# Grouped-query attention with a gated expert layer: the gate matrix in the start-up, earlier requests for the last weights, and the last output columns as separate products

## The chip, the cores and the metric

The kernel runs on one core of a Trainium2 chip. The core has five engines that each work through a queue of their own in order: TensorE (PE in the profile; its weight loads are PEld), VectorE (DVE), ScalarE (ACT), GpSimd (POOL) and SyncE (SP). Transfers run on sixteen DMA engines and are asked for by SyncE, ScalarE or GpSimd. The metric is the device time of one execution in microseconds (us). Before the change it is 369.04 us, the median of three runs (368.49 to 369.7).

## The reference

Attention over 8 batches of 384 positions, 16 query heads that share 4 key and value heads, 64 elements a head. Its output, regrouped to 3072 rows of 1024, goes into a two-stage gate: a row picks one of 4 groups and in it one of 4 experts, and is multiplied with that expert's two 1024 x 1024 matrices.

```python
scores = scale * np.matmul(q, k.transpose(0, 1, 3, 2))
attn = softmax(scores)                       # over the keys
x = np.matmul(attn, v)                       # then (batch, position) x 1024
g_idx = np.argmax(x @ w_group, axis=1)       # one of 4 groups
e_idx = np.argmax(xg @ w_expert[g], axis=1)  # one of 4 experts of the group
h = np.maximum(xg[mask_e] @ w1[g, e], 0.0)
out[tok_idx] = (g_w * e_w)[:, None] * (h @ w2[g, e])
```

## The kernel before

**Batches.** The eight batches run one after the other. For each batch `b` the kernel guesses one expert from the mean of v, loads that expert's two matrices `w1` and `w2` (4 MB each in float32, 2 MB each once they are cast to bf16 on the way), and computes the whole batch with it. Rows that chose another expert get weight zero and are left for a loop at the end, which runs once for each pair of a batch and an expert that is left over.

**Attention of a batch** (`Attn`) has 24 units: 4 key heads times 6 slices of the keys. In each unit TensorE computes scores of the unit after next (line 305), ScalarE takes the exp (line 311), TensorE multiplies with v (line 324), GpSimd adds pairs of exps (line 331) and VectorE reduces them to row sums (line 338). `run` takes a table of inserts: functions that are called after a given unit.

**The expert layer of a batch** has two halves. `moe_h(b, f0, ...)` computes two of the eight 128-column slices of the hidden layer (16 products, line 600) and ScalarE empties the tile (line 604). `ffn_y` and `y_out` compute the output (line 611), scale it with the rows' weights and store it. The layer of batch `b` runs after the attention of batch `b + 1`, in `block(b + 1)`; for batch 7 it stands alone at the end.

**Order of work.** The order is written out by hand: each engine does its work in the order in which the program names it. What matters here is the order in three queues.

- GpSimd: the adds of a batch's attention, then `prefetch(b)`: it reads the picked index (`pick`), makes a copy that waits until the q of batch `b + 1` has been transposed (`transposed`, line 667), and asks for `w1` (line 538) and `w2` (line 544) of batch `b`, then for k (line 92) and q (line 97) of batch `b + 2`.
- SyncE: the transposes by DMA of k and q of the next batch (lines 126, 128 and 120), loads of v (line 102), stores of results (lines 640 and 881).
- TensorE: its products in the order of the text.

There are two buffers each for `w1`, `w2` and v, and thirteen for the exps.

**Accumulator tiles.** `ps_tile` hands out four tiles of two banks: "s" and "o" each alternate between two, and "x" names the "o" tile that isn't the current one. A new product into a tile waits until the engine that reads the tile's old content is done.

**Start-up.** `first_scores` does warming products on a tile of ones (`fill`, line 268, 512 columns each), casts and transposes the first k and q on TensorE (lines 249 and 257), and copies them out. `gate_matrix_a` and `gate_matrix_b` bring the two gate matrices into the form that the gate needs: four transposes of float32 (line 221), two VectorE operations (lines 223 and 227), and later one product (line 232). Before the change part a stands after unit 3 of the attention of batch 0.

**The end.** The last loop over `c` computes three blocks of 128 rows, each as two halves of 512 columns. The very last half is emptied by ScalarE (256 columns, line 873) and VectorE (256 columns, line 874) and stored by SyncE and ScalarE (line 881).

Of the kernel before, what the change touches and what calls it, by code (L numbers as in the profile page):

```python
# [10 lines left out]
BF16 = mybir.dt.bfloat16  # L11
I32 = mybir.dt.int32
AX = mybir.AxisListType
ALU = mybir.AluOpType
# [4 lines left out]
def kernel(  # L19
# [11 lines left out]
    nc = tc.nc  # L31
# [39 lines left out]
    def ps_tile(which, shape=None, dtype=F32):  # L71
        if which == "x":
            which = f"o{1 - turn['o']}"
        else:
            turn[which] = 1 - turn[which]
            which += str(turn[which])
        return psum.tile(shape or [P, 2, 512], dtype, name="ps_" + which)
# [18 lines left out]
        qraw[b] = lpool.tile([P, KQ, NC * D], BF16, name="q_raw")  # L96
        nc.gpsimd.dma_start(out=qraw[b], in_=rows(q[b]))

    def load_v(b):
        vraw[b] = vpool.tile([P, Hkv, NC * D], F32, name="v_raw")  # L100
        for r in range(2):
            nc.sync.dma_start(out=vraw[b][r * H2:(r + 1) * H2],
                              in_=v[b].rearrange("h (p c) d -> p h (c d)", c=NC))

    def new_qT(b):
# [40 lines left out]
                              in_=v[0, g0:g1].rearrange("h (p c) d -> p h (c d)", c=NC))  # L146

    onesb = cpool.tile([P, 4 * P], BF16)
    nc.vector.memset(onesb, 1.0)
    nc.sync.dma_start(out=k0f[:, 0], in_=rows(k[0])[:, 0])  # L150
    for m in range(KG):
# [59 lines left out]
        nc.vector.tensor_scalar(eback, eidx, -1.0, float(NE - 1), op0=ALU.mult, op1=ALU.add)  # L211
        nc.vector.tensor_copy(out=pidx, in_=pback_i)

    gm = {}

    def gate_matrix_a(which):
        gm["pt"] = ps_tile(which, [P, 2, 512])
        pe = gm["pt"][:, 0, :Eg * 5 * KQ].rearrange("p (e n) -> p e n", e=Eg)
        wv = wraw.rearrange("a (p e) -> a e p", e=Eg)
        for e in range(Eg):  # L220
            nc.tensor.transpose(out=pe[:, e], in_=wv[:, e, :],
                                identity=id128f[:5 * KQ, :5 * KQ])
        nc.vector.tensor_copy(
            out=wg[:, :, :NW].rearrange("p k (a e) -> p e a k", e=Eg),
            in_=pe.rearrange("p e (a k) -> p e a k", k=KQ))
        pk = pe.rearrange("p e (a g t) -> p t g a e", a=5, t=KG)[:, 0]
        nc.vector.tensor_add(out=wgs.rearrange("p g (a e) -> p g a e", e=Eg), in0=pk,
                             in1=wg[:, 1::2, :NW].rearrange("p g (a e) -> p g a e", e=Eg))

    def gate_matrix_b():  # L230
        p2 = gm["pt"][:, 1, :Hkv * NW].rearrange("p (g n) -> p g n", n=NW)
        nc.tensor.matmul(out=p2, lhsT=mod64.rearrange("p a m -> p (a m)"), rhs=wgs,
                         start=True, stop=True)
        nc.vector.tensor_copy(out=wgd, in_=p2)
# [9 lines left out]
    def first_k(gp, which, eng):  # L244
        lo = gp * NC
        pt = ps_tile(which, [P, 16, P], BF16)
        for i in range(NC):
            for s in range(2):
                nc.tensor.transpose(out=pt[s * D:(s + 1) * D, i, :], in_=k16[0][:, lo + i],
                                    identity=id128b)  # L250
        evac(eng, kT[0][:, lo:lo + NC, :], pt[:, :NC, :])

    def first_q(i0, n, which, eng):
        pt = ps_tile(which, [P, 16, P], BF16)
        for i in range(n):
            a, c = (i0 + i) // SC, (i0 + i) % SC
            nc.tensor.transpose(out=pt[:, i, :], in_=qraw[0][:, a, c * P:(c + 1) * P],
                                identity=id128b)
        evac(eng, qT[0][:, i0:i0 + n, :], pt[:, :n, :])

    def first_scores():
        new_kT(0)
        new_qT(0)
        warm = ps_tile("o")

        def fill(n):
            for i in range(n):
                nc.tensor.matmul(out=warm[:, i % 2, :], lhsT=onesb[:, :P], rhs=onesb, start=True,  # L268
                                 stop=True)

        fill(8)
        nc.vector.tensor_copy(out=k16[0][:, :NC].rearrange("p c d -> p (c d)"), in_=k0f[:, 0])
        nc.scalar.copy(out=qraw[0][:, 0], in_=q0f[:, 0])
        nc.vector.tensor_copy(out=qraw[0][:, 1], in_=q0f[:, 1])
        first_k(0, "s", nc.vector)
        fill(2)
        first_q(0, SC, "s", nc.scalar)
        first_q(SC, SC, "o", nc.vector)
        fill(2)
        return fill  # L280

    def cast_k():
        nc.gpsimd.tensor_copy(out=k16[0][:, NC:NK].rearrange("p c d -> p (c d)"), in_=k0f[:, 1])
# [117 lines left out]
            out=rsum[b][:, g0:g1].rearrange("p g t j -> p g (t j)"),  # L401
            in_=reds[b][:, g0:g1].rearrange("p g n t j -> p g (t j) n"), axis=AX.X, op=ALU.add)

    def sums(b, g0, g1, which):
        sm = ps_tile(which, [P, Hkv, KG, NB])
        for r in range(2):
            for t in range(2):
                nc.tensor.matmul(out=sm[t * D:(t + 1) * D, g0:g1, r, :], lhsT=half32[:, r, :],  # L408
                                 rhs=rsum[b][:, g0:g1, t, :], start=True, stop=True)
        if b not in inv:  # L410
            inv[b] = gpool.tile([P, KQ, NB], F32, name="inv")
        nc.vector.reciprocal(out=inv[b][:, KG * g0:KG * g1],
                             in_=sm[:, g0:g1].rearrange("p g r j -> p (g r) j"))
# [213 lines left out]
    def moe_h(b, f0, which, mid=None):  # L627
        if f0 == 0:
            hTs[b] = xpool.tile([P, FQ, S], BF16, name="hT", bufs=1)
        ffn_h(xb[b], w1s[b], hTs[b], f0, which, mid)  # L630
# [14 lines left out]
    def do(f, *a):  # L645
        return lambda: f(*a)
# [1 line left out]


    gate_constants()  # L650
    fill = first_scores()
    index_constants()
    at = {0: Attn(0), 1: Attn(1)}
    at[0].start()
    fill(4)
    state, weights = {}, {}

    new_qT(1)
# [30 lines left out]
    def transposes(b):  # L689
        new_qT(b)  # L690
        trans_k(b)
        trans_q(b, 0, Hkv)
# [8 lines left out]
    def first_spread():  # L701
# [3 lines left out]
    a = at[0]  # L705
    a.run(0, NU, {
        1: [do(first_q, GB, GB, "x", nc.vector)],
        3: [cast_k, do(gate_matrix_a, "x")],
        4: [gate_matrix_b],
        6: [do(collect, 0, 0, 1)],  # L710
        7: [do(first_q, 2 * GB, 2 * GB, "x", nc.vector)],
# [22 lines left out]
        13: [do(cast, 0, 3)],  # L734
    })
    moe_h(0, 0, "s")
    load_v(2)
    transposes(2)
    pt = ps_tile("x")
    gate_logits(0, pt)  # L740
    guess_mean(1, pt)
    vm = mean_copy(pt, nc.scalar)
    moe_h(0, 2, "s", do(sums, 1, 0, 2, "s"))
    guess_logits(vm, pt)
    for m in range(2):
        normalise(1, m)
# [39 lines left out]
    def prefetch(b):  # L786
        if b != 2:
            pick(b)
        if b + 1 < B:
            transposed(b + 1)  # L790
        pick_w1(b)
        pick_w2(b)
        if b + 2 < B:
            loads(b + 2)

    def block(b):
        last = b == B - 1
        f = b - 1
        prefetch(b)
        moe_h(f, 0, "s")  # L800
        collect(b, 0, Hkv)
        weights[f]()
        out_weights(f)
        moe_h(f, 2, "s")
        sums(b, 0, Hkv, "o")
        for m in range(4):
            normalise(b, m)
        moe_h(f, 4, "s")
        moe_h(f, 6, "s")
# [12 lines left out]
        ffn_y(w2s[f], hTs[f], 1, "s", (1,), y)  # L822
        y_out(f, 1, y)
        if not last:
            guess_logits(vm, pt)
        weights[b] = gate_softmax(b, pt, not last)
        y = ffn_y(w2s[f], hTs[f], 2, "o", (0,))
        if not last:
            pick_index(b + 1)
            at[b + 1] = Attn(b + 1)  # L830
            y_scores(f, at[b + 1], y)
            return {}
        ffn_y(w2s[f], hTs[f], 2, "o", (1,), y)
        y_out(f, 2, y, nc.vector)
        weights[b]()
        out_weights(b)

    late = first_block()
    for b in range(2, B):
        if b + 1 < B:  # L840
            transposes(b + 1)
        at[b].run(0, NU, late)
        late = block(b)

# [17 lines left out]

    for c in range(SC):
        ot = opool.tile([P, DM], F32, name="ot")
        for nh in range(2):
            y = ps_tile("so"[nh])
            ffn_y(w2s[B - 1], hTs[B - 1], c, "", (nh,), y)
            sl = slice(nh * HALF, (nh + 1) * HALF)
            w = weff[B - 1][:, c:c + 1]
            if (c, nh) == (SC - 1, 1):  # L870
                q1 = slice(HALF, HALF + HALF // 2)
                q2 = slice(HALF + HALF // 2, DM)
                nc.scalar.mul(ot[:, q1], y[:, nh, :HALF // 2], w)
                nc.vector.tensor_scalar(ot[:, q2], y[:, nh, HALF // 2:], w, None, op0=ALU.mult)
            elif nh:
                nc.vector.tensor_scalar(ot[:, sl], y[:, nh, :], w, None, op0=ALU.mult)
            else:
                nc.scalar.mul(ot[:, sl], y[:, nh, :], w)
            for i, (ps, x) in enumerate(halves(c)):
                eng = nc.scalar if (c, nh, i) == (SC - 1, 1, 1) else nc.sync  # L880
                eng.dma_start(out=out_rows(out[(B - 1) * S:])[x][:, sl], in_=ot[ps, sl])
    region.close()

    n_left = nc.values_load(left_i[0:1, 0:1], min_val=0, max_val=B * NE)
# [72 lines left out]
```

The softmax here doesn't subtract the row's maximum and nothing guards it: scores larger than these inputs give would overflow.

## Time and profile before

| | value |
|---|---|
| time, median of three runs | 369.04 us |
| span of the profiled execution | 369.5 us |
| exp on ScalarE, 192 times | 814 ns each, 150.2 us |
| v products on TensorE (line 324), 1536 | 153.1 us busy |
| hidden-layer products (line 600), 480 on the "s" tiles | 81.1 us busy |
| weights asked for by GpSimd, 16 loads | 2048 KB each, median 22.6 us to landing |
| moved by DMA | 76.07 MB, mean 206 GB/s |

How to read it: busy time is summed over the span for each engine and says nothing of what waits for what. A line of the list of waits names the engine and the line that waited, after the arrow what ended the wait, then the total in microseconds, how often, and the longest. A line in order of time has start, duration, engine, source line, operation, tile written and tile read, and in brackets the idle time before it with what ended it. A row of a stretch of time gives each engine's busy time, then the granted TensorE clock, the busy share of the DMA engines (which can exceed 1, as transfers overlap) and what they moved in GB/s. In the chain that ended last each row is a start, a duration and the work that was followed back.

### The profile page before, as it was taken

Reading aid. Unit: us, or ns where it says so; the run is one execution under the profiler, and the core shown is the slowest. Engines: PE = TensorE matmul, PEld = TensorE weight load, DVE = VectorE, ACT = ScalarE, POOL = GpSimd, SP = SyncE. Lnnn points to the kernel's source line nnn. Section 1 sums busy time; section 2 is a strip of 40 time slices with the busy share of each in tenths; the row PEclk is TensorE's granted clock in tenths of the full one; section 3 lists DMA queues with packets and bytes.
Section 4 is the critical chain, followed back from the end, with each engine's and each line's share of the span. In section 5 each row is a group of like instructions: output and inputs, shape, how many; then the busy total and the mean of one; then the engine's idle time right before and its main releaser. Section 6 shows DMA issues by size and latency. Waiting matters only on the chain.

```text
span 369.5 us, 9587 instructions
## 1 busy us (share of the span) xinstructions
PE 357.0 (97%) x3984; PEld 185.7 (50%) x3999; DVE 259.2 (70%) x499; ACT 228.7 (62%) x300; POOL 150.0 (41%) x118
## 2 busy tenths in 40 slices
PE   8999999999999999999999999999999999999982
PEld 3545465455555455554555554554555545555530
DVE  4599799658976599747979379755997379793130
ACT  3889943749925596357944599355963589443221
POOL 6566960706803276034730377006750067500000
PEclk9999999999999999999999999999999999999997
DMA  8995999999999999999999999989999899999834
GB/s 195 247 105 88 241 213 159 248 235 287 219 155 201 256 263 211 131 201 285 234 208 154 259 261 213 193 134 243 281 212 186 157 227 240 212 212 266 230 76 98
DMA packets 71212, 76.07 MB, mean 206 GB/s; under 512 B 35928, under 2 KB 50264, under 8 KB 71168
## 3 DMA queue, kind: packets, MB, share of 16 engines
q0 software_dynamic: 26640, 41.03, 62.5%
q1 hardware_dynamic: 44096, 33.81, 37.6%
q8 instruction: 32, 0.52, 0.5%
q10 hardware_dynamic: 432, 0.61, 0.5%
q14 instruction: 12, 0.10, 0.1%
HBM read 89.21 MB, written 18.87 MB: 293 GB/s over the span
## 4 chain that ended last, share of the span: by engine, by line
PE 81%; DMA 9%; DVE 4%; ACT 2%; issue 1%; POOL 1%; POOLq 0%; ACTq 0%
PE ps_o L324 28%; PE ps_s L600 17%; PE ps_s L611 13%; DMA w<-in_moe_w_dram 9%; PE ps_s L305 8%; PE ps_o L611 7%; PE ps_o L444 3%; PE ps_o L268 2%; DVE red L338 1%; POOL e L331 1%; ACT e L311 1%; PE ps_o L408 1%; PE ps_o L454 1%; DVE ps_o L419 1%; DVE xT L428 1%
## 5 line engine op out<-in xcount | busy, mean ns | idle before, releaser
L311 ACT ACTIVATE e<-ps_s 128x768 f32<-128x768 f32 x192 | 150.2, 814 | 18.6 <-PE ps_s L305 15.6
L324 PE MATMUL ps_o<-e,v_raw 64*64 64x384 f32 x1536 | 153.1, 482 | 0.2 <-DVE xT L428 0.2
L331 POOL TENSOR_TENSOR e<-e 128x768 f32<-128x768 f32 x64 | 116.1, 1831 | 78.6 <-ACT e L311 54.4
L338 DVE TRANSPOSE_TENSOR_REDUCE red<-e 128x24 f32<-128x768 f32 x128 | 114.3, 947 | 18.3 <-POOL e L331 18.2
L600 PE MATMUL ps_s<-xb,w 128*128 128x384 bf16 x480 | 81.1, 326 | 1.0 <-ACT hT L604 0.8
L324 PEld LDWEIGHTS ps_o<-e,v_raw 64*64 64x64 f32 x1536 | 55.5, 133 | 37.4 <-issue 26.6
L600 PEld LDWEIGHTS <-w 128*128 128x128 bf16 x512 | 48.9, 98 | 36.7 <-issue 4.5
L305 PE MATMUL ps_s<-qT,kT 64*64 64x384 bf16 x768 | 63.7, 326 | 0.4 <-ACT e L311 0.2
L604 ACT ACTIVATE hT<-ps_s 128x768 bf16<-128x768 f32 x30 | 24.3, 810 | 62.0 <-PE ps_s L600 62.0
L611 PEld LDWEIGHTS <-hT 128*128 128x128 bf16 x384 | 36.0, 98 | 43.6 <-issue 3.6
L611 PE MATMUL ps_s<-w,hT 128*128 128x512 bf16 x234 | 54.6, 379 | 2.1 <-DMA w<-in_moe_w_dram 1.2
L305 PEld LDWEIGHTS <-kT 64*64 64x64 bf16 x768 | 24.4, 105 | 38.4 <-issue 36.7
L667 POOL COPY after<-qT 128x1 bf16<-128x1 bf16 x7 | 1.3, 192 | 86.4 <-DMA qT<-q_raw 83.5
L636 ACT ACTIVATE ot<-ps_s,we 128x1024 f32<-128x1024 f32 x14 | 15.6, 1114 | 27.3 <-PE ps_s L611 27.3
L611 PE MATMUL ps_o<-w,hT 128*128 128x512 bf16 x135 | 31.9, 379 | 0.1
L419 DVE STREAM_TRANSPOSE rb<-inv 128x384 f32<-128x384 f32 x60 | 31.0, 554 | 0.3
L428 DVE TENSOR_TENSOR xT<-xT,rb 128x768 f32<-128x768 f32 x25 | 24.0, 958 | 0.9
L240 ACT CAST xb<-xT 128x768 bf16<-128x768 f32 x27 | 21.1, 828 | 0.0
L374 DVE COPY xT<-ps_o 128x768 f32<-128x768 f32 x18 | 16.5, 919 | 0.0
L242 DVE CAST vm<-ps_o 128x4 bf16<-128x4 f32 x6 | 1.0, 161 | 21.0 <-PE ps_o L454 21.0
L638 DVE TENSOR_SCALAR ot<-ps_o,we 128x1024 f32<-128x1024 f32 x7 | 9.0, 1282 | 5.3 <-PE ps_o L611 5.1
L376 ACT COPY xT<-ps_o 128x768 f32<-128x768 f32 x10 | 8.0, 800 | 6.5 <-PE ps_o L324 6.5
(123 smaller groups left out, 181.3 us busy)
## 6 DMA issues: line engine op xcount, KB each, us to landing
w<-in_moe_w_dram POOLq DMA_DIRECT2D x16, 2048.0 KB, 22.6
out_dram<-ot SPq DMA_DIRECT2D x42, 256.0 KB, 7.8
xb_scratch<-xb SPq DMA_DIRECT2D x8, 768.0 KB, 10.2
q_raw<-in_q_dram POOLq DMA_DIRECT2D x7, 768.0 KB, 34.4
v_raw<-in_v_dram SPq DMA_DIRECT2D x14, 384.0 KB, 5.9
out_dram<-ot SPq DMA_DIRECT2D x11, 128.0 KB, 2.3
k<-in_k_dram POOLq DMA_DIRECT2D x7, 192.0 KB, 31.4
w<-in_q_dram POOLq DMA_DIRECT2D x3, 192.0 KB, 6.6
```

The lines of the kernel that those rows point to most:

```text
L240: eng.copy(out=out_, in_=in_)
L305: nc.tensor.matmul(out=sT[r * H2:(r + 1) * H2, s, :S], lhsT=kT[b][s * D:(s + 1) * D, slot, ks], rhs=qT[b][s * D:(s + 1) * D, kq * SC:(kq + ...
L311: nc.scalar.activation(e.rearrange("p t (s x) -> p s t x", s=2), sT[:, :, :S].rearrange("p s (t x) -> p s t x", t=2), ACT.Exp, scale=scale)
L324: nc.tensor.matmul(out=oT[t * D:(t + 1) * D, r, :S], lhsT=vraw[b][r * H2:(r + 1) * H2, g, c * D:(c + 1) * D], rhs=self.e[u][r * H2:(r + 1) ...
L331: eng.tensor_add(out=self.e[u], in0=self.e[u], in1=self.e[u + 1])
L338: nc.vector.tensor_reduce(out=reds[self.b][:, g, n].rearrange("p t j -> p (t j)"), in_=self.e[u].rearrange("p t (j x) -> p (t j) x", x=32) ...
L374: nc.vector.tensor_copy(out=dst, in_=src)
L419: nc.vector.transpose(out=rb[:, r].rearrange("p (j x) -> p j x", x=32), in_=inv[b][:, 2 * m + r].unsqueeze(2).to_broadcast([P, NB, 32]))
L428: eng.tensor_mul(out=x, in0=x, in1=rb)
L600: nc.tensor.matmul(out=h[:, jj, :S], lhsT=w1[:, kq, (f0 + jj) * P:(f0 + jj + 1) * P], rhs=x[:, kq, :], start=(kq == 0), stop=(kq == KQ - 1))
L604: nc.scalar.activation(hT[:, f0:f0 + 2, :], h[:, :, :S], ACT.Relu)
L611: nc.tensor.matmul(out=y[:, nh, :], lhsT=hT[:, f, c * P:(c + 1) * P], rhs=w2[:, f, nh * HALF:(nh + 1) * HALF], start=(f == 0), stop=(f == ...
```

## The change

It does five things.

1. **Start-up.** A second, smaller tile of ones (128 columns) is set first, and four products of 128 columns on it and six of 512 take the place of eight of 512. The fills between and after the transposes are three instead of four. ScalarE instead of VectorE copies out the first keys, VectorE instead of ScalarE the first queries. The idea is to have the first scores sooner.
2. **Gate matrix.** Part a moves from after unit 3 of batch 0 to directly after the first two scores, where four warming products stood, so that useful work keeps TensorE busy there.
3. **Row sums.** `sums` takes a piece of a tile that is handed in. For the first half of batch 1 that is the gate's tile, so no "s" tile is used up between two calls of `moe_h`.
4. **Requests.** v of batch 2 is asked for by GpSimd instead of SyncE, and the weights of batch 7 at the head of that batch's attention instead of after it.
5. **The end.** The last 512 columns become two groups of 256 with products of their own. VectorE empties the first, ScalarE the second, and SyncE stores both.

```diff
+    ones1 = cpool.tile([P, P], BF16)
+    nc.vector.memset(ones1, 1.0)
...
-        fill(8)
+        for i in range(4):
+            nc.tensor.matmul(out=warm[:, i % 2, :P], lhsT=ones1, rhs=ones1, start=True, stop=True)
+        fill(6)
...
-        first_k(0, "s", nc.vector)
-        fill(2)
-        first_q(0, SC, "s", nc.scalar)
+        first_k(0, "s", nc.scalar)
+        first_q(0, SC, "s", nc.vector)
+        fill(1)
         first_q(SC, SC, "o", nc.vector)
         fill(2)
...
     at[0].start()
-    fill(4)
+    gate_matrix_a()
...
-        3: [cast_k, do(gate_matrix_a, "x")],
+        3: [cast_k],
...
-    load_v(2)
+    load_v(2, nc.gpsimd)
...
-    moe_h(0, 2, "s", do(sums, 1, 0, 2, "s"))
+    moe_h(0, 2, "s", do(sums, 1, 0, 2, pt))
...
     def block(b):
...
-        prefetch(b)
+        if not last:
+            prefetch(b)
...
         if b + 1 < B:
             transposes(b + 1)
+        else:
+            prefetch(b)
         at[b].run(0, NU, late)
...
-        for nh in range(2):
-            y = ps_tile("so"[nh])
-            ffn_y(w2s[B - 1], hTs[B - 1], c, "", (nh,), y)
...
+        parts = [(0, HALF), (HALF, DM)]
+        if c == SC - 1:
+            parts = [(0, HALF), (HALF, 3 * HALF // 2), (3 * HALF // 2, DM)]
+        for i, (n0, n1) in enumerate(parts):
+            y = ps_tile("so"[i % 2])
+            for f in range(FQ):
+                nc.tensor.matmul(out=y[:, 0, :n1 - n0], lhsT=hTs[B - 1][:, f, c * P:(c + 1) * P],
+                                 rhs=w2s[B - 1][:, f, n0:n1], start=(f == 0), stop=(f == FQ - 1))
...
+            for ps, x in halves(c):
+                nc.sync.dma_start(out=out_rows(out[(B - 1) * S:])[x][:, n0:n1], in_=ot[ps, n0:n1])
```

More of the change, by code (lines that the diff above doesn't have):

```diff
@@ L97, in load_q, with load_v @@
         nc.gpsimd.dma_start(out=qraw[b], in_=rows(q[b]))
-    def load_v(b):
+    def load_v(b, eng=nc.sync):
         vraw[b] = vpool.tile([P, Hkv, NC * D], F32, name="v_raw")
         for r in range(2):
-            nc.sync.dma_start(out=vraw[b][r * H2:(r + 1) * H2],
+            eng.dma_start(out=vraw[b][r * H2:(r + 1) * H2],
                               in_=v[b].rearrange("h (p c) d -> p h (c d)", c=NC))
@@ L212, in index_constants, with gate_matrix_a @@
         nc.vector.tensor_copy(out=pidx, in_=pback_i)
[L214 to L218, printed above, removed]
+    def gate_matrix_a():
+        pe = ps_tile("o")[:, 0, :Eg * 5 * KQ].rearrange("p (e n) -> p e n", e=Eg)
         wv = wraw.rearrange("a (p e) -> a e p", e=Eg)
@@ L230, in gate_matrix_b @@
     def gate_matrix_b():
-        p2 = gm["pt"][:, 1, :Hkv * NW].rearrange("p (g n) -> p g n", n=NW)
+        p2 = ps_tile("x")[:, 1, :Hkv * NW].rearrange("p (g n) -> p g n", n=NW)
         nc.tensor.matmul(out=p2, lhsT=mod64.rearrange("p a m -> p (a m)"), rhs=wgs,
@@ L274, in first_scores @@
         nc.vector.tensor_copy(out=qraw[0][:, 1], in_=q0f[:, 1])
-        first_k(0, "s", nc.vector)
-        fill(2)
-        first_q(0, SC, "s", nc.scalar)
+        first_k(0, "s", nc.scalar)
+        first_q(0, SC, "s", nc.vector)
+        fill(1)
         first_q(SC, SC, "o", nc.vector)
         fill(2)
-        return fill
     def cast_k():
@@ L402, in collect, with sums @@
             in_=reds[b][:, g0:g1].rearrange("p g n t j -> p g (t j) n"), axis=AX.X, op=ALU.add)
-    def sums(b, g0, g1, which):
-        sm = ps_tile(which, [P, Hkv, KG, NB])
+    def sums(b, g0, g1, pt):
+        if isinstance(pt, str):
+            pt = ps_tile(pt)
+        sm = pt[:, 1, 128:128 + Hkv * KG * NB].rearrange("p (g r j) -> p g r j", r=KG, j=NB)
         for r in range(2):
@@ L650 @@
     gate_constants()
-    fill = first_scores()
+    first_scores()
     index_constants()
@@ L864 @@
         ot = opool.tile([P, DM], F32, name="ot")
-        for nh in range(2):
-            y = ps_tile("so"[nh])
-            ffn_y(w2s[B - 1], hTs[B - 1], c, "", (nh,), y)
[L868 to L876, printed above, removed]
-            else:
[L878 to L881, printed above, removed]
+        w = weff[B - 1][:, c:c + 1]
+        parts = [(0, HALF), (HALF, DM)]
[6 more added lines that the diff above has]
+                                 rhs=w2s[B - 1][:, f, n0:n1], start=(f == 0), stop=(f == FQ - 1))
+            if i % 2:
+                nc.vector.tensor_scalar(ot[:, n0:n1], y[:, 0, :n1 - n0], w, None, op0=ALU.mult)
+            else:
+                nc.scalar.mul(ot[:, n0:n1], y[:, 0, :n1 - n0], w)
+            for ps, x in halves(c):
+                nc.sync.dma_start(out=out_rows(out[(B - 1) * S:])[x][:, n0:n1], in_=ot[ps, n0:n1])
     region.close()
```

## The prediction

> **What bounds the kernel now.** I read the shares of the page first, then the waits, then GpSimd's order of time, then how long each load took to land, then the chain. The shares and the waits:
>
> ```profile
> PE 357.0 (97%) x3984; PEld 185.7 (50%) x3999; DVE 259.2 (70%) x499; ACT 228.7 (62%) x300; POOL 150.0 (41%) x118
> ...
> POOL after L667 <- DMA qT<-q_raw: 83.5, 6, 20.4
> ...
> PE ps_s L611 <- DMA w<-in_moe_w_dram: 1.2, 1, 1.2
> PE ps_s L600 <- ACT hT L604: 0.8, 1, 0.8
> ...
> SPq L102 <- PE ps_s L305: 6.2, 1, 6.2
> ```
>
> TensorE (PE) is at work 97% of the span and hardly waits: 1.6 us at the start, 0.8 us once at L600, 1.2 us once at L611. But GpSimd waits six times, 83.5 us in all, for the transposed q of the next batch (L667), and only after that copy does it ask for a batch's weights. In order of time:
>
> ```profile
> 70.25 0.19 POOL L667 COPY after<-qT 128x1 bf16<-128x1 bf16 x1 [0.69 <-DMA qT<-q_raw]
> 70.92 0.91 POOL L538 DMA_DIRECT2D w<-in_moe_w_dram  x1 [0.49 <-issue]
> ...
> 115.43 0.19 POOL L667 COPY after<-qT 128x1 bf16<-128x1 bf16 x1 [13.08 <-DMA qT<-q_raw]
> ...
> 294.91 0.22 POOL L667 COPY after<-qT 128x1 bf16<-128x1 bf16 x1 [20.39 <-DMA qT<-q_raw]
> 295.52 0.92 POOL L538 DMA_DIRECT2D w<-in_moe_w_dram  x1 [0.39 <-issue]
> ```
>
> From batch 1 to 6 the asks lie (295.52 - 70.92) / 5 = 44.9 us apart, while the chain has TensorE's batches 43.04 us apart (first L600 products at 102.27, 145.31, 188.35 us). The wait of the copy grows from 0.69 to 20.39. So there are two loops, and the transfers are the slower by 1.9 us a batch. The slack, from each load's time to landing against the first product that reads it (w1: L600, w2: L611):
>
> | batch | w1 lands, is read | w2 lands, is read |
> |---|---|---|
> | 1 | 93.6, 102.2 | 103.3, 112.9 |
> | 3 | 182.8, 188.3 | 192.8, 199.0 |
> | 5 | 271.9, 274.4 | 282.5, 285.1 |
> | 6 | 315.4, 317.4 | 326.4, 328.1 |
> | 7 | 336.3, 340.0 | 352.1, wanted at 350.7 |
>
> The slack shrinks from 9 us to nothing, and the last w2 comes 1.4 us late. Here the chain turns into a transfer:
>
> ```profile
> 318.41 33.72 DMA w<-in_moe_w_dram
> 352.13 0.04 issue
> 352.17 0.38 PE ps_s L611
> ```
>
> That row starts at the ask, but the ask didn't bound it. By stretch of time:
>
> ```profile
> 320.00:325.00 5.00, 5.00 (x38) 2.97 (x36) 3.11 (x10) 1.73 (x3) 0.00 (x0) 1.00 1.12 212
> ```
>
> The last two columns, DMA share 1.12 and 212 GB/s, stay near that from 305 to 345 us. Batch 6's w2 landed at 326.4, batch 7's w1 at 336.3, 9.9 us later for 2 MB: 212 GB/s, one after the other with no gap, though w1 was asked for at 317.5. **The end is bound by when the stream of weights began, not by the last ask.**
>
> **What the Trainium skill says.** "DMA: Bandwidth & Descriptors", Queues, rings and completion order: each DMA engine takes descriptors of a ring in order and goes round the rings that have work. The trace agrees: GpSimd's loads land in the order asked, and share only with SyncE's. The same page, SWDGE vs HWDGE vs iDMA: one queue is allocated for GpSimd's DMAs, so batch 7's weights asked for sooner stand behind batch 6's. "TensorE: Matmul & The Clock Gate", Part 1: TensorE starts at half clock and is released after some 3.4 us of work. The trace agrees: eight warming products take 3.60 us, four at 8.29 us take 1.04.
>
> **The change, part by part.**
>
> Start. Before, the first keys' transposes (L249) begin at 5.13, when the eight warming products are through, though the cast they read was done at 4.23. Now four 128-column products and six of 512. The small ones wait for a 128-column memset (0.2 us, by the 0.17 of a like one) instead of 0.48, so begin near 1.3; 4 x 0.11 + 6 x 0.43 = 3.0 us (a quarter of a cold 512 each), to 4.3. Keys' and first q's transposes follow; the second q's cast ends at 5.28 as before (its DMA); one fill and three transposes, to 6.35; DVE copies it out to 6.7. The keys' copy is ACT's now, 0.80 us (L376) instead of 0.56, 5.2 to 6.0, beside the q work. Two fills end near 6.95, and scores start there instead of 7.80: 0.85 us (0.4 to 1.1).
>
> Gate matrix. Its four transposes stood after unit 3 of attention 0: scores at 12.28 and next at 13.78, 1.50 us against the usual 0.81, so 0.69 us leaves the path. Now they stand where four fills stood, while TensorE waits for the first exp; their 0.67 us is less than the fills' 1.04, and the raw gate lands near 6.2, in time. DVE's two copies (0.68 us) move with them into idle DVE time (0.80 to 3.20 us idle there). Cost: nothing.
>
> Start and gate: 1.54. One cap: batch 0's ask stands behind the copy at 31.01, which waits for DVE's index but also for batch 1's q transposes, issued at 26.72 with 2.8 us to land: 29.5. So at most **1.5 us**. From there to 48.9 the chain runs over GpSimd adds, DVE reduces and ACT exps that stand behind this ask, and moves with it.
>
> Sums into the gate's tile. Before, the row sums of batch 1 took an "s" tile between two moe_h calls, so that the third found the second's tile not yet emptied:
>
> ```profile
> 57.48 2.76 PE L600 MATMUL ps_s<-xb,w 128*128 128x384 bf16 x16 [0.81 <-ACT hT L604]
> ```
>
> Now it gets the first's, emptied at 52.5: **0.8 us**. The sums' new tile has its mean already copied out (53.70, a microsecond earlier). Sum for TensorE: 2.3 us.
>
> v of batch 2 by GpSimd. Before, SyncE waits 6.2 us for the buffer, asks at 34.12, and 0.79 MB runs beside batch 0's w1, which takes 16.7 us to land where 2 MB alone take 9.9. Now it stands behind q of batch 2 in GpSimd's queue; its two issues (0.9 each at GpSimd's rate) fall into an idle stretch of 13.6 us. Batch 0's weights and batch 2's k and q land sooner, k near 53 instead of 59.3, so its transposes are done near 64 to 66, before GpSimd's last add of batch 1 (69.56 - 2.3 = 67.2). The 0.69 us wait at 70.25 goes, 0.2 of it lost to the copy's own order: batch 1's ask moves 2.3 + 0.5 = **2.8 us**, and the stream behind it with it (2.3 if the wait stays; to 3.7 if batch 0's x, stored at 68.47 beside that stream, goes earlier too).
>
> Batch 7's asks at the head. Queue order is the same, so w2 gains nothing by it: 0. Queued behind them on GpSimd are the adds of attention 7, which DVE's reduces wait for: index load and two issues, first add at some 300.6 instead of 299.41, 1.2 us. Adds take 3.62 of each 4.84 us, so the next group is on time; DVE (4.48 of 4.84) recovers 0.36 a group and ends attention some 0.1 to 0.2 late, with 0.7 us free before the collect is wanted.
>
> Last columns. TensorE does sixteen products of 256 columns for eight of 512: 109 ns each by the skill's page on TensorE, Back-to-back issue gap (weight loads, 98, fit under it), against 216 measured: nothing. ACT and DVE no longer copy one after the other (0.47, then 0.48), but SyncE issues four stores where SyncE and ACT issued one each. SyncE is busy to 362.87, issues lie 0.52 to 0.64 apart: the last starts near 364.65 instead of 363.75 and lands in 2.2 instead of ACT's 3.0, near 366.8 as before. Bounds -0.5 and +0.6; I take 0.
>
> Sum: TensorE wants w2 at 350.7 - 2.3 = 348.4, it lands at 352.1 - 2.8 = 349.3, a wait of 0.9. The end moves by 2.8: 369.04 - 2.8 = **366.2 us**. Batch 6 keeps its 1.7 us of slack, as its stream moves no less than TensorE.
>
> **The rivals.**
> - The ask was the bound, or the stream moves by 3.7: no wait for w2, 2.3 + 1.4 = 3.7, so 365.3. For: the chain draws the transfer from the ask. Against: batch 6's w2 and batch 7's w1 land without a gap.
> - The clock comes a window later, as transposes stand where products stood: 3.4 us at half rate lose up to 1.7 of the first 1.5; sums and v keep 1.3, so 367.7. For: ten transposes more among fewer fills. Against: TensorE is not idle longer.
> - The stream doesn't move: only TensorE comes sooner and waits longer, 369.0. For: 33.7 us of DMA in the chain. Against: it starts at 70.92, behind adds that TensorE paces.
> - GpSimd blocks on its queue: rows outstanding were at most 1024 + 1024 + 256 + 1024 = 3328 (w1, w2, k, q); now near 4096. Nothing shows a limit; were it just there, 768 rows at 102 a us block the adds for 7.5 us; the 13 exp tiles cover part of it, some 5 us reach TensorE: 371.2, slower than before.
>
> **Chances.** Forecast 0.52, asked-sooner 0.16, late clock 0.11, stream fixed 0.10, GpSimd blocked 0.11. Faster 0.79, same 0.10, slower 0.11. The range goes from 364.8 (start bound 1.1, all waits gone) to 369.2 (stream fixed), leaving out mainly the blocked case.
>
> **What would show it.** First exp near 7.5 instead of 8.24; no wait of L600 for L604 near 57; batch 1's ask near 68.1 without a wait for qT; about 44.9 us between asks; batch 7's w1 asked near 297 but landing near 333.5, w2 near 349.3, L611 waiting near 1 us. Wrong if w2 lands before 347 (the ask counted) or if GpSimd's DMA rows grow past 1 us near 297.

## The result and the profile after

The changed kernel takes **370.77 us** (median of 4 runs, 370.23 to 371.22) against 369.12 us (368.49 to 369.7) for the kernel before on the same chip: a ratio of 1.0044, 95% interval 1.0023 to 1.0066. It is 1.65 us slower. The forecast was 366.2 with a range of 364.8 to 369.2: the change went the other way. Device time is 1.6 to 2.0 us above the span of the profile in every run here. The two profiles must not be set against each other at their ends: the execution profiled before the change took 371.23 us (span 369.5), the one after it 370.23 (span 368.5), so the first was a late execution of the faster kernel.

In the changed kernel most of the lines have moved down: 600 is now 602, 604 is 606, 611 is 613, 667 is 669, 538 and 544 are 540 and 546. The last loop over `c` has products of its own (877), emptied by VectorE (880) and ScalarE (882) and stored by SyncE (884). First the shares and the list of waits, as in the prediction:

```profile
PE 355.1 (96%) x3989; PEld 186.4 (51%) x4004; DVE 259.4 (70%) x500; ACT 229.0 (62%) x300; POOL 151.3 (41%) x120
...
POOL after L669 <- DMA qT<-q_raw: 106.1, 7, 22.0
...
PE ps_s L877 <- DMA w<-in_moe_w_dram: 1.6, 1, 1.6
```

TensorE's 0.8 us wait for ScalarE is gone, as planned, but its wait for the last w2 is 1.6 us instead of 1.2. GpSimd's wait for the transposed q has grown from 83.5 to 106.1 us. GpSimd in order of time shows where that begins (start, duration, engine, line, work, and in brackets the idle time before):

```profile
29.41 0.19 POOL L669 COPY after<-qT 128x1 bf16<-128x1 bf16 x1 [3.50 <-DMA qT<-q_raw]
...
50.44 1.29 POOL L102 DMA_DIRECT2D v_raw<-in_v_dram  x2
...
71.14 0.19 POOL L669 COPY after<-qT 128x1 bf16<-128x1 bf16 x1 [4.18 <-DMA qT<-q_raw]
71.75 0.92 POOL L540 DMA_DIRECT2D w<-in_moe_w_dram  x1 [0.43 <-issue]
...
118.01 0.19 POOL L669 COPY after<-qT 128x1 bf16<-128x1 bf16 x1 [18.25 <-DMA qT<-q_raw]
...
297.41 0.88 POOL L540 DMA_DIRECT2D w<-in_moe_w_dram  x1 [1.55 <-DVE ot L640]
298.42 0.87 POOL L546 DMA_DIRECT2D w<-in_moe_w_dram  x1
299.31 1.83 POOL L331 TENSOR_TENSOR e<-e 128x768 f32<-128x768 f32 x1
```

Batch 0's ask is 1.6 us sooner than before, as forecast. Batch 1's was to come at 68.1 without a wait; it comes at 71.75, after a wait of 4.18 us, and is **later than before** (70.92), although GpSimd was ready 2.6 us sooner (66.96 for 69.56, the copy's start less its wait). The slack, worked out as in the prediction:

| batch | w1 lands, is read | w2 lands, is read |
|---|---|---|
| 1 | 94.1, 99.6 | 104.2, 110.5 |
| 3 | 183.2, 185.7 | 192.7, 196.6 |
| 5 | 271.6, 271.8 | 281.5, 282.7 |
| 6 | 313.5, 315.0 | 323.4, 325.9 |
| 7 | 334.3, 337.8 | 350.2, wanted at 348.6 |

TensorE is 2.1 to 2.6 us ahead of the first profile from batch 1 on. The loads of batches 1 to 5 are not: they land within about 1 us of the first profile's times, on either side. Batch 1 has 5.5 us of slack instead of 8.6. Those of batches 6 and 7 land 1.9 to 3.0 us sooner than in the first profile, but later than in a second profile of the kernel before (the first experiment), where the last four land at 312.0, 322.0, 332.1 and 348.5. The end of the chain, and the last issue of interest:

```profile
348.37 0.22 PE ps_o L854
348.58 1.58 another core or an unknown queue
350.17 0.04 issue
350.21 0.38 PE ps_s L877
```

```profile
L884 SPq DMA_DIRECT2D out_dram<-ot x1: 1389/1389/1389, 362.2 to 362.2; - x1
```

The first row that isn't TensorE's is the wait for w2 (the list of waits names the transfer). The second fence is one store of 64 KB by SyncE, which took 1.389 us to issue where its neighbours took 0.55 to 0.59. From the end of the last product to the end of the span there are 7.78 us; before, there were 6.77.

So there are two losses to explain: a stream of weights whose second ask came no sooner, and an end that is 1.0 us longer.

### The profile page after: what moved, and what is told of

It reads as the page before. It is cut to its first block, busy times and chain, and to the rows that moved or that the text cites. A ratio compares the mean times of both kernels' runs of the same rounds, so it can differ in the third digit from the quotient of the medians.

```text
span 368.5 us, 9604 instructions
## 1 busy us (share of the span) xinstructions
PE 355.1 (96%) x3989; PEld 186.4 (51%) x4004; DVE 259.4 (70%) x500; ACT 229.0 (62%) x300; POOL 151.3 (41%) x120
## 4 chain that ended last, share of the span: by engine, by line
PE 88%; DVE 6%; ACT 2%; issue 1%; POOL 1%; another core or an unknown queue 0%; POOLq 0%; ACTq 0%
PE ps_o L324 27%; PE ps_s L602 22%; PE ps_s L613 13%; PE ps_s L305 8%; PE ps_o L613 7%; PE ps_o L446 3%; DVE red L338 3%; PE ps_s L877 2%; PE ps_o L602 1%; PE ps_o L877 1%; ACT e L311 1%; PE ps_o L410 1%; PE ps_o L267 1%; DVE xT L430 1%; PE ps_o L456 1%
## 5 line engine op out<-in xcount | busy, mean ns | idle before, releaser
L311 ACT ACTIVATE e<-ps_s 128x768 f32<-128x768 f32 x192 | 150.2, 814 | 18.7 <-PE ps_s L305 15.8
L613 PE MATMUL ps_s<-w,hT 128*128 128x512 bf16 x211 | 49.0, 379 | 0.9 <-issue 0.2
L613 PEld LDWEIGHTS <-hT 128*128 128x128 bf16 x336 | 31.3, 98 | 36.6 <-issue 2.1
L669 POOL COPY after<-qT 128x1 bf16<-128x1 bf16 x7 | 1.4, 200 | 106.1 <-DMA qT<-q_raw 106.1
L613 PE MATMUL ps_o<-w,hT 128*128 128x512 bf16 x111 | 26.3, 379 | 0.1
```

What stands on the lines that cost most here:

```text
L311: nc.scalar.activation(e.rearrange("p t (s x) -> p s t x", s=2), sT[:, :, :S].rearrange("p s (t x) -> p s t x", t=2), ACT.Exp, scale=scale)
L613: nc.tensor.matmul(out=y[:, nh, :], lhsT=hT[:, f, c * P:(c + 1) * P], rhs=w2[:, f, nh * HALF:(nh + 1) * HALF], start=(f == 0), stop=(f == ...
```

## The experiments

Each kernel ran against the kernel before on the same chip. The theory: v of batch 2, moved to GpSimd's queue, delays the stream, and the last columns lengthen the end. The rivals: the requests of batch 7 or GpSimd's queue do harm; the start-up brings nothing; the difference is scatter of the stream from one execution to the next. The ratios below compare each kernel with the kernel before over many executions; they are not the quotients of the two medians shown.

| kernel | median us (before) | executions | ratio, 95% interval |
|---|---|---|---|
| before, repeated | 369.55 (369.61) | 14 | 1.0002 [0.999, 1.0013] |
| changed, repeated | 370.35 (369.61) | 22 | 1.0034 [1.0012, 1.0057] |
| before + v by GpSimd | 372.79 (369.59) | 11 | 1.006 [1.003, 1.0091] |
| changed, v by SyncE again | 368.74 (369.61) | 22 | 0.9986 [0.9971, 1.0002] |
| before + v behind k and q | 370.41 (369.6) | 22 | 1.0027 [1.001, 1.0045] |
| before + last columns | 370.55 (369.59) | 11 | 1.0025 [1.0014, 1.0037] |
| changed, old last columns | 370.51 (369.61) | 22 | 1.0022 [1.0007, 1.0037] |
| last columns, last store by ScalarE | 369.88 (369.6) | 13 | 1.0006 [0.9997, 1.0015] |
| before + sums | 369.07 (369.6) | 14 | 0.999 [0.9973, 1.0006] |
| before + start-up, gate, sums | 367.79 (369.59) | 11 | 0.9962 [0.9943, 0.9982] |
| the same + batch 7's requests | 367.71 (369.59) | 6 | 0.9958 [0.9944, 0.9971] |
| the same, v behind k and q | 368.92 (369.6) | 22 | 0.9987 [0.9972, 1.0001] |

A profile shows one execution, and some of those profiled were late ones of their kernel: 374.24 us with v by GpSimd alone, 370.43 with v by SyncE again, 373.31 and 370.94 with v behind k and q, 372.33 with the sums alone. The changed kernel's second profile was an early one, 368.67. The others lie within 1.2 us of their medians.

### The kernel before and the changed one, again

No edit in either.

> The kernel before against itself, to see how far its time, its profile and the start of its weight stream scatter. All theories: ratio 1.000 within 0.003. Theory 'late stream': batch 1's ask between 70.5 and 71.5 us, the last w2 lands about 1 to 2 us after TensorE wants it. Theory 'the profile of before was an odd one': the span of this run lies 1 us or more below the 369.5 us of the first profile, with no wait of the first L611 products for w2.

> The changed kernel again, all five parts. Theory 'late stream': TensorE reaches the last w2 about 2.5 us sooner than before and waits 2 us for it, because batch 1's ask is no sooner than before (near 71.5). Theory 'tail': from the first product that reads the last w2 to the end of the span 18.2 us against 17.3 before. Together ratio 1.000 to 1.005; if the slower time was one chip's scatter, 0.993 to 0.998.

The kernel before repeats at 1.0002. Its new profile, though, differs from the one that the prediction was built on: a span of 367.7 us instead of 369.5, w2 of batch 7 landing at 348.5, 2.0 us before TensorE reads it at 350.5, and no wait of L611 in the list. The execution profiled first took 371.23 us, when the median is 369. **The wait of 1.2 us that the prediction took for the state of the kernel was that of one late execution.** In the three profiles here that keep the old start and the old stream (this one, and the two below with only the last columns changed) the last w2 lands 1.0 to 2.7 us ahead of its product.

The changed kernel is slower again, 1.0034, with single executions from 368.14 to 373.55. In its second profile batch 1's ask is at 70.98, again no sooner than before (70.92 and 70.74), and TensorE waits 0.5 us for the last w2.

### v of batch 2 by GpSimd

Alone on the kernel before:

```diff
-    def load_v(b):
+    def load_v(b, eng=nc.sync):
...
-    load_v(2)
+    load_v(2, nc.gpsimd)
     transposes(2)
```

> The kernel before with one part of the change: v of batch 2 asked for by GpSimd, behind q of batch 2. Theory 'v delays the stream': batch 0's w1 lands 3 us sooner (near 45), but kT's two transposes of batch 2 take over 6.5 us of SyncE's time instead of 4.8, batch 1's ask moves from 70.7 to 71 or later, the last w2's slack falls from about 2 to 0 us, and the time rises by 0.5 to 2 us (ratio 1.001 to 1.006). Theory 'v is harmless': ask within 0.5 us of 70.7, ratio 0.998 to 1.001.

Ratio 1.006: some 2.2 us slower, alone. SyncE in order of time, first in the kernel before (the repeated one), then with v by GpSimd:

```profile
58.95 0.52 SPq L126 DMA_DIRECT2D k<-k  x1
59.51 4.90 SPq L128 DMA_TRANSPOSE kT<-k  x2
64.52 3.66 SPq L120 DMA_TRANSPOSE qT<-q_raw  x1
```

```profile
58.58 0.51 SPq L126 DMA_DIRECT2D k<-k  x1
59.19 7.46 SPq L128 DMA_TRANSPOSE kT<-k  x2
66.74 3.70 SPq L120 DMA_TRANSPOSE qT<-q_raw  x1
```

SyncE copies k as soon as it has landed: at 58.58 instead of 58.95, 0.4 us sooner and not the 6 of the forecast. Then the two transposes of k take 7.46 us of SyncE instead of 4.90, since the second waits for the 16 KB copy of k, and q's are issued 2.2 us later. SyncE's list of waits has the wait for that copy, before and then with v (the longest is the last number):

```profile
SPq L128 <- DMA k<-k: 17.2, 7, 3.3
```

```profile
SPq L128 <- DMA k<-k: 20.8, 7, 5.1
```

How GpSimd's copy sees it, before and with v:

```profile
70.06 0.19 POOL L667 COPY after<-qT 128x1 bf16<-128x1 bf16 x1 [0.81 <-DMA qT<-q_raw]
```

```profile
74.06 0.19 POOL L667 COPY after<-qT 128x1 bf16<-128x1 bf16 x1 [4.77 <-DMA qT<-q_raw]
```

The ask is 4.0 us later: 2.2 by the later issue, the rest because q's transposes land 7.3 us after it instead of 5.5. What the DMA engines moved in that time, before and then with v (the last two columns are DMA share and GB/s):

```profile
42.00:47.00 5.00, 4.81 (x76) 2.84 (x71) 4.90 (x7) 4.98 (x8) 4.99 (x5) 1.00 1.12 237
...
58.00:64.00 6.00, 6.00 (x52) 3.36 (x51) 5.48 (x21) 2.24 (x4) 0.00 (x0) 1.00 1.09 147
```

```profile
42.00:47.00 5.00, 4.81 (x76) 2.84 (x72) 4.90 (x7) 4.98 (x8) 4.98 (x5) 1.00 1.05 174
...
58.00:64.00 6.00, 6.00 (x53) 3.34 (x51) 5.48 (x21) 2.20 (x3) 0.00 (x0) 1.00 1.32 219
```

From 42 to 47 us, beside batch 0's w1, SyncE's v had brought the total to 237 GB/s; without it GpSimd's loads don't speed up to fill the room, and the stretch moves 174. The trace has 411 of their 2048-byte packets start in it with v beside them, 416 without. w1 of batch 0 lands 2.5 us sooner (45.6 for 48.1), but w2, whose ask at 42.1 stands behind GpSimd's adds, only 0.3 sooner (57.6 for 57.9), and k and q stand behind w2 in the queue. From 58 to 64, where the transposes of k and q run, v brings the rate from 147 to 219. The Trainium skill, "DMA: Bandwidth & Descriptors", Queues, rings and completion order, has each DMA engine go round the queues packet by packet. The trace agrees: in 59 to 64 us packets of v (4608 bytes, some 320 ns each) run beside those of the copy of k, which begins near 62 instead of 60 and is done near 64 instead of 62. The other profiles with v by GpSimd have the long row too: k's two transposes take 7.27 and 8.05 us of SyncE in the two of the changed kernel. The kernel that differs from the changed one in v and the last columns alone (the last one below) has 4.71. The changed kernel's second profile, then that one:

```profile
56.64 8.05 SPq L128 DMA_TRANSPOSE kT<-k  x2
```

```profile
58.83 4.71 SPq L128 DMA_TRANSPOSE kT<-k  x2
```

Its ask of batch 1 is at 69.88, those of the changed kernel are at 71.75 and 70.98. With v alone by GpSimd the end follows: w2 of batch 7 lands at 354.4 instead of 348.5, and TensorE waits for it:

```profile
PE ps_s L611 <- DMA w<-in_moe_w_dram: 2.6, 1, 2.6
```

Undone in the changed kernel, with the other four parts kept:

```diff
-    load_v(2, nc.gpsimd)
+    load_v(2)
```

> The changed kernel with v of batch 2 asked for by SyncE again, all else as changed. Theory 'late stream' (v behind q slows the transposes of batch 2 and so delays batch 1's ask): the ask moves from 71.7 to near 68.5, kT's two transposes take under 5.5 us of SyncE's time instead of 7.3, the last w2 lands 2 us sooner or more, and the time falls by 1.5 to 3 us against all five parts. Theory 'tail alone': under 0.5 us.

0.9986 against 1.0034 for the repeated changed kernel: 0.48% or 1.8 us back, the same size as alone. In its profile the kT row is undisturbed (q's transposes are issued at 64.80), but batch 1's ask is no sooner, 71.04, and the last w2 lands at 349.7, neither of which fits the expectation. The execution is a late one, and its loss lies elsewhere: the q transposes of batch 1 landed near 31.8, so batch 0's ask came at 32.5, GpSimd's adds behind it came later as well, and TensorE waited for the row sums that need them:

```profile
39.44 0.42 PE L410 MATMUL ps_o<-rsum,half 128*64 128x24 f32 x8 [3.27 <-DVE rsum L400]
```

In the changed kernel's own profiles this wait is 0.9 and 1.0 us.

### v asked for by SyncE, but later

To tell "v collides with the transposes" from "v must come early", SyncE asks for v behind the transposes of k and q, in the kernel before and in the best kernel (below):

```diff
-    load_v(2)
     transposes(2)
+    load_v(2)
```

> The kernel before with v of batch 2 still asked for by SyncE, but behind the transposes of k and q of batch 2. It no longer runs beside batch 0's w1, as with GpSimd, but not beside the transposes either. Theory 'v behind q is bad because it runs beside the copy and the transposes of k': k is copied near 57, q transposed near 67, batch 1's ask falls to the end of its adds (near 70.2 or before), and the time is 0 to 0.8 us below before. Theory 'v must come early': it collides with v of batch 3 and x of batch 0 near 69 to 75 us, batch 1's w1 lands later than 93, and the time rises by 0.5 us or more.

> Start-up, gate, sums and batch 7's asks of the change, last columns as before, and v of batch 2 by SyncE behind the transposes. Theory 'v behind q is bad because of the transposes': batch 1's ask near 68.5, the last w2 lands by 347, TensorE doesn't wait, and the time is 366.5 to 367.7, no worse than the 367.7 with v in its old place. Theory 'v must come early': 368.2 or more.

The first is slower, 1.0027; the second loses most of its kernel's gain (0.9987 for 0.9958). The transposes are undisturbed now, and in the first kernel batch 1's ask is as soon as before (70.20). In the profile of the second it comes at 71.12 instead of 69.88, but that execution has the same late row sums as above (TensorE waits 2.9 us for them), so it doesn't show what v does. SyncE's order of time in the first kernel reads:

```profile
63.93 3.73 SPq L120 DMA_TRANSPOSE qT<-q_raw  x1
67.76 1.36 SPq L102 DMA_DIRECT2D v_raw<-in_v_dram  x2
69.22 0.54 SPq L751 DMA_DIRECT2D xb_scratch<-xb  x1
69.86 2.43 SPq L102 DMA_DIRECT2D v_raw<-in_v_dram  x2
```

v of batch 2, x of batch 0 and v of batch 3 now go out in one row, just when batch 1's weights are asked for. w1 of batch 1 lands at 95.9 instead of 92.6, and the next ask is at 119.7 instead of 115.6. **So it isn't only the collision with the transposes.** v by GpSimd and v behind the transposes both bring w1 of batch 1 in 3 to 4 us late (96.5 and 95.9). My estimate: 0.79 MB at the stream's 212 GB/s are 3.7 us. Beside batch 0's w1 they cost the stream nothing that counts, as batch 0's w2 has 11 us of slack; from 55 us on they cost it about their length.

### The last columns

Alone on the kernel before:

```diff
+        parts = [(0, HALF), (HALF, DM)]
+        if c == SC - 1:
+            parts = [(0, HALF), (HALF, 3 * HALF // 2), (3 * HALF // 2, DM)]
...
+            for ps, x in halves(c):
+                nc.sync.dma_start(out=out_rows(out[(B - 1) * S:])[x][:, n0:n1], in_=ot[ps, n0:n1])
```

> The kernel before with one part of the change: the new last columns. Theory 'tail': 0.7 to 1.0 us more between the end of the last L611 product and the end of the span (7.5 instead of 6.7), and the time rises by the same (ratio 1.002 to 1.003), since nothing lies behind it. Theory 'tail is a wash': ratio within 0.001 of 1.

1.0025, some 0.9 us slower; 7.36 us from the last product to the end instead of the 6.69 of the repeated kernel before. The third of SyncE's four small stores takes 1.29 us to issue here too (shortest, median and longest of its last six):

```profile
L879 SPq DMA_DIRECT2D out_dram<-ot x6: 467/588/1294, 360.5 to 364.3; - x6
```

Undone in the changed kernel (the old loop put back):

```diff
-            for i, (n0, n1) in enumerate(parts):
+            for nh in range(2):
...
+                eng = nc.scalar if (c, nh, i) == (SC - 1, 1, 1) else nc.sync
```

> The changed kernel with the old last columns (one half of 512, emptied by ScalarE and VectorE, stored by SyncE and ScalarE), all else as changed. Theory 'tail' (four stores in SyncE's queue cost more than the two copies one after the other): 0.7 to 1.1 us faster than all five parts. Theory 'late stream alone': within 0.4 us of all five parts.

Only 1.0022 against 1.0034, 0.4 us, with intervals that overlap. Its profile has the short end, 6.75 us, but its stream came late in the middle (batch 1's ask at 72.3, 0.8 and 0.9 us of slack for w1 of batches 4 and 5). A part of 1 us isn't measured well in a kernel whose time the stream scatters by 5. A cleaner pair is the one without v by GpSimd: 0.9986 with the new columns, 0.9958 with the old, 1.0 us.

Then the new products with the very last store on ScalarE's queue:

```diff
-                nc.sync.dma_start(out=out_rows(out[(B - 1) * S:])[x][:, n0:n1], in_=ot[ps, n0:n1])
+                eng = nc.scalar if i == 2 and ps.start else nc.sync
+                eng.dma_start(out=out_rows(out[(B - 1) * S:])[x][:, n0:n1], in_=ot[ps, n0:n1])
```

> The kernel before with the new last columns, but the very last store issued by ScalarE instead of SyncE. Theory 'SyncE's queue of stores is what the new end costs': one issue of 0.6 us leaves it, and the tail from the last L611 product to the end of the span falls from 7.4 to 6.6 to 6.9 us, the ratio from 1.0025 to 0.9995 to 1.001. Theory 'small stores land late whatever issues them': tail stays above 7.1, ratio 1.002 or more.

1.0006, no slower than before by its interval, and 6.98 us from the last product to the end. The stores at the end:

```profile
361.80 0.54 ACTq L880 DMA_DIRECT2D out_dram<-ot  x1
```

```profile
L880 SPq DMA_DIRECT2D out_dram<-ot x5: 466/587/1560, 360.3 to 362.7; - x5
```

SyncE's long issue is still there (the longest of five is 1560 ns, the usual 587), but nothing stands behind it. So most of the loss is the queue of four stores on one engine (0.38 of 0.67 us in these profiles, and 1.0006 for 1.0025 in time); the two groups of products cost nothing that can be measured, and bring nothing either.

### What was left over: start-up, gate, sums, batch 7's requests

Sums alone on the kernel before:

```diff
-    def sums(b, g0, g1, which):
...
+    def sums(b, g0, g1, pt):
...
-    moe_h(0, 2, "s", do(sums, 1, 0, 2, "s"))
+    moe_h(0, 2, "s", do(sums, 1, 0, 2, pt))
```

> The kernel before with one part of the change: the row sums of batch 1 in the gate's tile. Both theories: the wait of the hidden-layer products for the tile (0.8 us near 57 us) goes and TensorE runs 0.8 us ahead from there. Theory 'the stream sets the end': the time falls by 0.3 to 0.8 us, as far as the last w2's slack allows (ratio 0.998 to 0.9995). Theory 'passes through': 0.8 us (0.9978).

0.999, with an interval that holds 1. In the profiled execution, the longest of its 14, TensorE is 0.7 to 0.8 us ahead of the repeated kernel before from 60 to 230 us, loses that again in two waits for a transposed q (0.8 us in all), and waits 2.2 us for the last w2, which lands at 353.0. The time hardly moves.

Start-up, gate matrix and sums together, v, batch 7's requests and last columns as in the kernel before:

```diff
-        fill(8)
+        for i in range(4):
+            nc.tensor.matmul(out=warm[:, i % 2, :P], lhsT=ones1, rhs=ones1, start=True, stop=True)
+        fill(6)
...
-    fill(4)
+    gate_matrix_a()
...
-    moe_h(0, 2, "s", do(sums, 1, 0, 2, "s"))
+    moe_h(0, 2, "s", do(sums, 1, 0, 2, pt))
```

> The kernel before with the start-up, the gate matrix and the row sums of the change; v, batch 7's asks and the last columns as before. Theory 'the stream sets the end': TensorE runs 2.3 us ahead of before, but the last w2 lands near 348.5 to 350.5 as before, so only 0.5 to 1.5 us of it show (ratio 0.996 to 0.999) and the first product that reads the last w2 waits in most executions. Theory 'the gain passes through': ratio 0.993 to 0.995.

0.9962, 1.4 us faster. The copy in GpSimd's order of time:

```profile
69.34 0.19 POOL L669 COPY after<-qT 128x1 bf16<-128x1 bf16 x1 [1.81 <-DMA qT<-q_raw]
```

GpSimd is ready 1.7 us sooner than in the repeated kernel before (69.34 - 1.81 against 70.06 - 0.81), the copy comes 0.7 us sooner: the transposes, the later of the two already, now hold the copy up longer. The last w2 lands at 348.4, 0.4 us before TensorE reads it at 348.8, which is 1.7 us sooner than in the repeated kernel before.

With batch 7's requests at the head of its attention as well:

```diff
+        if not last:
+            prefetch(b)
...
+        else:
+            prefetch(b)
         at[b].run(0, NU, late)
```

> As the one before it, with batch 7's asks at the head of its attention as well (start-up, gate, sums and asks; v and last columns as before). Theory 'the asks stand in queue and change nothing': within 0.3 us of the kernel without the asks. Theory 'asked sooner, landed sooner': the last w2 lands 1 us sooner or more and the time falls by as much. Theory 'the asks hold up GpSimd's adds': attention 7 takes 43.3 us or more instead of 43.04 and the time rises by 0.2 to 0.5 us.

0.9958, which the intervals don't part from 0.9962. w1 and w2 are asked for at 297.3 and 298.3, 18 us sooner than without this part, and land at 330.9 and 346.6, 2.0 and 1.8 us sooner: behind batch 6's in the same queue, which land 2.2 and 1.5 us sooner too in this profile. In it no line of `PE ps_s L613 <- DMA` is left, and w2 is there 2.3 us before it is read. **This is the best kernel of the study**: 367.71 us (367.18 to 368.3, only 6 executions), 1.6 us under the kernel before by the ratio.

## Why the prediction was wrong

**Right, in the main.** TensorE's 2.3 us held in the first pair of profiles: the last hidden-layer product starts at 348.04 instead of 350.46. L600's wait is gone, and sums alone put TensorE 0.8 us ahead. The first exp comes 0.85 us sooner, which is the forecast's figure for the first scores, if one takes the medians of seven profiles with the old start-up (7.66) and seven with the new one (6.81); the 8.24 of the first profile was a late one. Batch 7's requests bring nothing beyond the intervals, their loads land in the order of the queue, and attention 7 took 43.2 us in one profile of the changed kernel and 43.0 in the other, against 43.04. GpSimd didn't block on its queue: its two issues near 297 took 0.88 and 0.87 us, so that rival falls, although it named nearly the time measured (371.2 for 370.77). The clock didn't come late either: in seven profiles with the new start-up the transposes ran at their full rate by 6.2 us.

**Right, but too small: the cap of the start.** That batch 1's q transposes bound the copy is so: they let it go at 29.41 in the first profile after, for 29.5 in the forecast. They don't land at a fixed time, though. The first hidden-layer product of batch 0 starts at 48.4 to 49.0 us in the seven profiles with the old start-up, at 47.2 to 47.9 in five with the new one, and at 49.7 and 50.8 in two, where the copy stood until 31.87 and 31.71. So start-up and gate are worth about 0.9 us of the 1.5 (the medians are 48.8 and 47.9).

**Wrong, the step that cost most: "batch 1's ask moves 2.3 + 0.5 = 2.8 us".** It moved 0.8 us the other way, and in the second profile of the changed kernel it stayed where it was (70.98). "k near 53 instead of 59.3" took it that v's bytes leave a gap which the loads behind fill at once. It was 57.55 and 56.02 in the two profiles; with v alone moved it came 0.4 us sooner. w1 of batch 0 took 14.2 us to land without v beside it, where the forecast went from 16.7 toward 9.9, and w2 landed 15.5 us after its ask for 15.8 with v. And "its transposes are done near 64 to 66" left out that v, now last in the queue, runs beside just these transposes, which lengthened SyncE's row for k from 4.76 to 7.27 us. So the wait for qT, 0.69 us before, was 4.18 us instead of gone. Alone this part costs 0.6% or 2.2 us where the forecast had a gain of 0.5.

**Wrong: last columns, "I take 0".** The term that was mis-sized is SyncE's issues. The last was to start 2.0 us after the last product's end (364.65 - 362.69); it started 2.9 after it (363.68 - 360.75), 0.8 of the difference being the third issue, 1.39 us for 0.6. Its landing, 2.2 in the forecast, was 2.0 us where only this part was changed. The end is 1.0 us longer, outside the bounds of -0.5 to +0.6.

**Wrong: the arithmetic of the end.** "At 352.1 - 2.8 = 349.3, a wait of 0.9" starts from a wait that was seen in one execution of 371.23 us, and its gain is then taken off the median of 369.04. With w2 2.0 us ahead of its use, as in the repeated profile, a stream that goes sooner gains nothing, and TensorE's own gain is the most there is. Start-up, gate and sums brought 1.4 us of time, and in that profile TensorE reads the last w2 1.7 us sooner without waiting for it: the rest of the 2.3 was mostly lost at the cap above, not to the stream.

That w2 landed at 350.2 and TensorE waited 1.6 us for it, near the 349.3 and 0.9 of the forecast, is luck. Batch 1's ask was 0.8 us later and not 2.8 sooner; the stream made up for it between batches 1 and 6, whose asks lie 44.5 us apart, as in the repeated kernel before (44.4), where the first profile had 44.9.

The parts add up: -1.4 (start-up, gate, sums), 0 (requests), +2.2 (v; 1.8 in the changed kernel), +0.9 (last columns) make +1.7, against 1.65 measured first and 1.3 by the ratio of the repetition. They were measured on different chips and aren't independent: with the old last columns v costs 2.4 us (1.0022 against 0.9958), with the new ones 1.8. The rival "the stream doesn't move", 369.0, was nearest to the picture of the stream, without the two costs.

**Open.** Why the stream's times scatter from one execution to the next (the last w2 between 346.6 and 354.4 in these profiles); why batch 1's q transposes let GpSimd's copy go at 29.3 us in one execution and at 31.9 in another; why SyncE's third small store takes 1.2 to 1.6 us to issue; why 42 to 47 us move only 174 GB/s without v, and what sets the 15.5 us of batch 0's w2. Start-up and gate weren't run apart.

## What to carry to other kernels

A transfer moved to another queue isn't gone: ask where its bytes ran before and what slack the loads beside it had, then where they will run, and what small transfers on the path stand there. Where two loops, the engine's and the stream's, run within a few microseconds of each other, a gain of one turns into a wait for the other, and a single profile can show the wrong one as the bound; take a second profile of the unchanged kernel before building a sum on a wait of a microsecond. At the very end count the stores that stand on one queue: in this kernel four stores on two queues ended sooner than four on one.

## What the runs showed of the hardware that was not expected

- GpSimd's queue alone (float32 cast to bf16 on the way) moved 201 to 215 GB/s from 47 to 52 us in four profiles, but 173 and 174 from 42 to 47 in two; with a load of SyncE's beside it the sum from 42 to 47 was 237 and 241.
- Three transposes and a 16 KB copy took 4.0 us longer in all with 0.79 MB of another queue's traffic beside them (v by GpSimd alone). In the two profiles of the changed kernel the k row alone grew by 2.6 and 3.3 us over the 4.71 of the kernel that differs in v and the last columns alone, and q's transposes landed 5.7 and 5.6 us after their issue, near the usual 5.5.
- The third store of 64 KB in a row on SyncE took 1.22 to 1.56 us to issue in all five profiles that have the new last columns (in one of them the fourth is ScalarE's), the others 0.54 to 0.60.
- TensorE reaches its full rate at a moment that differs from execution to execution: 4.9 to 7.3 us after the start of the span in seven profiles with the old start-up, 4.7 to 6.2 in seven with the new one (read from transposes of 0.22 instead of 0.31 us). The Trainium skill, "TensorE: Matmul & The Clock Gate", Part 1, puts it down to a free-running window of some 3.4 us and gives the moment a scatter of 500 ns either way; the 2.4 us measured here are more than that, though less than one window. The prediction had taken it for a fixed time.
